# Sums of w_in on VectorE, and the last four rows' states made together from 64-row products

## The chip, the cores and the metric

The kernel runs on one core of a Trainium2 chip. The metric is the device time of one execution in microseconds. The kernel before takes 1135.21 us as the median of three runs (1133.67 to 1135.47). The engines are TensorE (PE in the rows; its weight loads are PEld), VectorE (DVE), ScalarE (ACT), GpSimd (POOL) and SyncE (SP), which issues every DMA here.

## The reference

Attention of every batch row between 512 tokens and 32 states, in both directions, then two feed-forward layers over all 8 x (512 + 32) = 4608 tokens.

```python
B, H, S, Ns, D = (8, 8, 512, 32, 64)
a     = softmax(x @ state.T * scale);   xread = a @ state       # token rows
a2    = softmax(state @ x.T * scale);   sread = a2 @ x          # state rows
x     = concat([xread, sread]) as (4608, 512)
# layer 1: d_ff 1536
gate  = 1.0 / (1.0 + np.exp(-(x @ w_gate)));  val = x @ w_val
x     = (gate * val) @ w_out
# layer 2: d_ff 1024
h     = x @ w_in
solu  = h * softmax(h)
ln    = (solu - mean) / sqrt(var + 1e-06) * g_ln
out   = ln @ w_out2
```

The weights come as 64-bit floats and are turned into 32-bit ones on the chip. A 32-bit operand of a large product is split into a high and a low half, and the product is the sum of three: high by high, low by high, high by low (`mm3`, lines 137 to 140).

## The kernel before

Layer 1 goes through nine token blocks: batch rows 0 to 6, then all 256 state tokens together (the state row, `SREAD`), then batch row 7, the last row. Each block has 12 chunks of 128 hidden units (loop at line 1037). A chunk is 12 products for gate and val into the banks `gps` and `vps` (`first_mm`), a sigmoid on ScalarE (`sigma`), the product of both on VectorE (`gated`), its split into `gh` and `gl`, and 12 products by `w_out` into four banks (`out_acc`), one chunk late. Beside it, attention of the next row runs in ten parts (`attention`); chunk 4 holds its exponentials (`exps`), which switch ScalarE's table and back.

A token row needs no product by w_gate of full depth. Since xread is a by state, `state_w` makes state by weights (256 x 3072 per row) in 12 steps, each 128 x 512 of gate and val of two chunks, and `first_mm` multiplies that by the attention weights. From row 2 on, rows go in pairs (`paired`): while the even row of the pair is made, six products of 128 rows a step (three for each of two groups `k` of 128 weight rows) make both rows' states. Their stationary operand holds two heads and two rows by 32 states, with the two heads' halves swapped between rows. Half of a result belongs to the other row, is copied to SBUF (`spill`) and stored to DRAM (`msp`); the odd row loads its steps from there (`state_load`) and only splits them (`put`). `make` issues a step in each chunk, two or three chunks ahead of use; `loads` issues the loads up to three steps ahead.

The order within this part is the order of the code (`manual_schedule`); each engine runs its own list in that order, and SyncE likewise its DMAs. In the state row `Conv` turns w_in into halves `xe`, `xo`; in the last row it does the same for w_out2 (`conv.step`, lines 1077 and 1078: ScalarE, three VectorE operations, one GpSimd addition `L223`, then a split at `L235`). Also in the last row, two steps a chunk of `w_pair_ops` form T1 to T4 from w_in: `do_join` adds the halves, `do_sub` subtracts, `do_split` splits, all on GpSimd but for the high half on ScalarE.

Layer 2 then runs over 34 tiles of 128 tokens in pairs (lines 1128 to 1180), seven products a pair instead of eight. `turn` transposes a tile through DRAM, `halves` splits it when it has come back, `out2` multiplies by w_out2, `store` writes. In the first pair, ScalarE meets `halves` ahead of the copies of products 5 and 6. In the last pair product 4 overwrites the bank that VectorE's `plus` (line 1164) reads, and that `plus` stands behind `chain(i)`.

The lines printed next are those that the profile names.

Of the kernel before, what the change touches and what calls it, by code (L numbers as in the profile page):

```python
# [9 lines left out]
F32 = mybir.dt.float32  # L10
# [4 lines left out]
ALU = mybir.AluOpType  # L15
# [3 lines left out]
WARM = 11  # L19
EXPS = 7  # L20

EXP_LO = 2.0 ** -15
# [4 lines left out]
def attn_moe_moe2_kernel(ctx: ExitStack, tc: tile.TileContext, x, state, w_gate, w_val, w_out, w_in2, w_out2, g_ln, out):  # L27
# [88 lines left out]
    ysp = [tc.dram_tile([KC, P, S if b < B else SR], F32, name=f"ysp{b}") for b in range(B + 1)]  # L116
    ssp = tc.dram_tile([B, P, KC * NS], F32, name="ssp")
    msp = [tc.dram_tile([NF1, P, 512], F32, name=f"msp{b}") for b in range(B)]

# [171 lines left out]
    def paired(a):  # L291
        return 2 <= a < B and a - a % 2 + 1 < B

# [213 lines left out]
    def state_w(b, p, g, i, o, hi, o2=vps):  # L507
# [3 lines left out]
        s = spill[n % 4]  # L511
        if not paired(b):
# [3 lines left out]
        elif b % 2 == 0:  # L516

            for q, o in enumerate((gps, o2)):
                k = 2 * g + q
                mm3(o, sth[:, k, :], stl[:, k, :], wpart(xe, p, k), wpart(xo, p, k), True, True)  # L520
                own = slice(64 * q, 64 * q + 64)
                other = slice(64 - 64 * q, 128 - 64 * q)
                hi(h[own], o[own])
                hi(s[other], o[other])
                lo_of(l[own], o[own], h[own])
            for q in range(2):
                nc.sync.dma_start(out=msp[b + 1][n, 64 - 64 * q:128 - 64 * q], in_=s[64 * q:64 * q + 64])
        else:
            put(s, h, l, hi)

    def state_load(b, n):
        nc.sync.dma_start(out=spill[n % 4], in_=msp[b][n])

# [37 lines left out]

    def out_acc(c, n):
        h, l = woh[c], wol[c]
        i = c % 2
        for m in range(KC):
            sl = slice(m * P, (m + 1) * P)
# [59 lines left out]
    def w_pair_ops(bf):  # L636

        join, sub, split = [{} for _ in range(3)]
        for k in range(2):
            b = dict(zip(("B11", "B12", "B21", "B22"), bf[4 * k:4 * k + 4]))  # L640

            def do_join(n, k=k, b=b):
                h, l = win(k + 2 * (n[1] == "2"), int(n[2]) - 1)
                pool.tensor_tensor(out=b[n], in0=r(h), in1=r(l), op=ALU.add)

            def do_sub(o, x, y, b=b):
                pool.tensor_tensor(out=b[o], in0=b[x], in1=b[y], op=ALU.subtract)
# [13 lines left out]
        for k in range(2):  # L661
            steps += late[:1] + [join["B11", k], join["B12", k], sub["T1", k], join["B22", k], split["T1", k], sub["T3", k]]
            steps += [sub["T2", k], join["B21", k], split["T3", k], split["T2", k], sub["T4", k]]
            late = [split["T4", k]]
# [11 lines left out]
    def h2_out(i, f):  # L676
        if tiles[i][0] == 0:
            return acc[2 * (i % 2) + f]
        a, b, c = banks(i)
        return ((b, c), (a, b))[i % 2][f]  # L680

# [138 lines left out]
    def make(n=1, o=gps, hi=hi_of, o2=vps):  # L820
        nonlocal made
        while n and made - NF1 < len(ring) and made - used < 3:
            state_w(*ring[made - NF1], made, o, hi, o2)
            made += 1
            n -= 1

    def loads(n):

        nonlocal loaded
        loaded = max(loaded, made - NF1)  # L830
        while loaded < min(made - NF1 + n, len(ring)):
            b, p, g = ring[loaded]
            if not paired(b) or b % 2 == 0:
                return
# [175 lines left out]
    with tc.manual_schedule():  # L1010
        for n_b, b in enumerate(blocks[1:], 1):
# [5 lines left out]
            if last:  # L1017
# [7 lines left out]
                y_load(1)  # L1025
                x_late.close()
                sbt = ctx.enter_context(tc.tile_pool(name="sbt", bufs=1, side="right"))
                for w in ("T1", "T2", "T3", "T4"):
# [6 lines left out]
                w_steps = w_pair_ops([sbf.tile([P, 512], F32, name=f"bf{i}") for i in range(8)])  # L1035
            nxt = blocks[n_b + 1] if not last else None
            for c in range(NF1):
                pe, others = parts[c] if c < len(parts) else (None, None)
# [14 lines left out]
                make(1, hi=hi, o2={3: vps, 4: vps, 7: vps, 9: att[0]}.get(c, att[1]))  # L1053
                if c > 0:
                    out_acc(c - 1, n)
                else:
                    out_acc(NF1 - 1, n_before)
# [21 lines left out]
                if last:  # L1079
                    for _ in range(2):  # L1080
# [46 lines left out]
    with tc.manual_schedule():  # L1127
        for i in range(len(first), nt, 2):
# [15 lines left out]
            h_max(i, 0)  # L1144
            halves(i - 2, 0)
            halves(i - 2, 1)
            row_scale(i - 2)
# [16 lines left out]
            plus(v, o, tmp)  # L1164
            h_max(i + 1, 1)
            centre(i)
# [57 lines left out]
```

## Time and profile before

| | before |
|---|---|
| median of three runs | 1135.21 us |
| the profiled execution's own time | 1134.19 us |
| its span, first to last instruction | 1132.4 us |
| mean granted TensorE clock | 0.994 |
| TensorE busy | 1084.0 us (96%) |
| VectorE busy | 766.7 us (68%) |
| ScalarE busy | 601.8 us (53%) |
| GpSimd busy | 418.7 us (37%) |

A row of a timeline gives the start in us, the duration in us, the engine, the line, the operation, output<-inputs and a count; what stands in brackets is idle time before it and who ended it. Products overlap: their durations are longer than the distance between their starts, so a stretch is read from starts.

### The profile page before, as it was taken

How to read it: one execution, taken by the hardware profiler on the slowest of the kernel's cores; microseconds unless marked ns; L12 is line 12 of the kernel's file. 1: busy time of each engine (PE TensorE's matmuls, PEld its weight loads, DVE VectorE, ACT ScalarE, POOL GpSimd, SP SyncE). 2: the span in 40 equal slices, each digit the busy share in tenths (PEclk: the TensorE clock that was granted, in tenths of full speed). 3: DMA queues.
4: the chain of work that ended last, by engine and by line, in shares of the span. 5: the costliest groups of instructions: out<-in, count | busy, mean ns of one | idle time of the engine just before them, and what ended most of it. 6: DMA issues, size and time to landing. Idle time of an engine off the chain costs nothing.

```text
span 1132.4 us, 15911 instructions
## 1 busy us (share of the span) xinstructions
PE 1084.0 (96%) x5501; PEld 861.5 (76%) x5501; DVE 766.7 (68%) x1324; ACT 601.8 (53%) x1169; POOL 418.7 (37%) x469
## 2 busy tenths in 40 slices
PE   7887899999999999999999999889999999999998
PEld 5555567778878778778778997667788888888877
DVE  6999865467465575564574466877578778777773
ACT  6766445545444455443555354555565565655552
POOL 2776733300000000000000054676566667667550
PEclk9999999999999999999999999999999999999999
DMA  8763040331440431532412434311453543553431
GB/s 230 258 204 102 20 95 1 80 84 38 116 124 20 115 66 38 164 77 58 96 38 67 142 99 149 106 39 56 134 174 121 174 155 131 164 170 119 158 122 38
DMA packets 139601, 122.89 MB, mean 109 GB/s; under 512 B 71040, under 2 KB 111232, under 8 KB 139520
## 3 DMA queue, kind: packets, MB, share of 16 engines
q1 hardware_dynamic: 139520, 121.87, 36.8%
q8 instruction: 43, 0.70, 0.3%
q14 instruction: 38, 0.31, 0.1%
HBM read 78.32 MB, written 43.52 MB: 108 GB/s over the span
## 4 chain that ended last, share of the span: by engine, by line
PE 73%; DVE 14%; issue 3%; DMA 3%; POOL 2%; ACT 2%; SPq 1%; DVEq 0%; POOLq 0%; ACTq 0%
PE acc L138 10%; PE acc L140 10%; PE acc L139 10%; PE att L138 5%; PE att L140 5%; PE att L139 5%; PE gps L138 4%; PE gps L139 4%; PE gps L140 4%; PE vps L138 4%; PE vps L140 4%; PE vps L139 4%; DVE wf L213 2%; DVE wf L203 1%; DVE wf L206 1%
## 5 line engine op out<-in xcount | busy, mean ns | idle before, releaser
L138 PE MATMUL acc<-gh,woh 128*128 128x512 f32 (+1 forms) x432 | 168.7, 390 | 0.6 <-ACT gh L129 0.6
L564 DVE TENSOR_TENSOR sg<-vps,sg 128x512 f32<-128x512 f32 (+1 forms) x108 | 71.1, 658 | 141.7 <-PE vps L140 123.0
L139 PE MATMUL acc<-gl,woh 128*128 128x512 f32 (+1 forms) x432 | 164.6, 381 | 2.2 <-POOL gl L570 1.3
L140 PE MATMUL acc<-gh,wol 128*128 128x512 f32 (+1 forms) x432 | 164.3, 380 | 0.0
L560 ACT ACTIVATE sg<-gps 128x512 f32<-128x512 f32 (+1 forms) x108 | 61.6, 570 | 154.5 <-PE gps L140 150.0
L138 PEld LDWEIGHTS acc<-gh,woh 128*128 128x128 f32 x432 | 81.8, 189 | 31.9 <-issue 15.5
L256 POOL MEMSET xtr<- 32x256 f32 x18 | 5.4, 302 | 262.1 <-PE att L324 261.5
L139 PEld LDWEIGHTS acc<-gl,woh 128*128 128x128 f32 x432 | 81.9, 190 | 18.5 <-POOL gl L570 2.2
L775 POOL TENSOR_TENSOR wol<-ut,woh 128x512 fp32r<-128x512 f32 x48 | 61.6, 1299 | 87.7 <-ACT woh L129 85.8
L140 PEld LDWEIGHTS acc<-gh,wol 128*128 128x128 f32 x432 | 81.6, 189 | 16.1
L223 POOL TENSOR_TENSOR tt<-tt,xn 128x512 int32<-128x512 int32 x16 | 20.9, 1304 | 194.8 <-DVE tt L213 171.2
L129 ACT ACTIVATE gh<-sg 128x512 fp32r<-128x512 f32 (+1 forms) x101 | 60.5, 599 | 53.6 <-DVE sg L564 53.6
L138 PE MATMUL gps<-ah,mh 128*128 128x512 f32 x192 | 75.9, 396 | 9.3 <-ACT sg L560 4.1
L570 DVE TENSOR_TENSOR gl<-sg,gh 128x512 fp32r<-128x512 f32 (+1 forms) x97 | 76.3, 786 | 10.2 <-ACT gh L129 6.9
L135 DVE TENSOR_TENSOR ml<-gps,mh 64x512 fp32r<-64x512 f32 (+2 forms) x57 | 38.6, 678 | 63.1 <-ACT stg L129 51.0
L138 PE MATMUL att<-woh,woh 128*128 128x512 f32 (+1 forms) x204 | 80.1, 392 | 0.0
L139 PE MATMUL att<-wol,woh 128*128 128x512 f32 (+1 forms) x204 | 79.5, 390 | 0.0
L140 PE MATMUL att<-woh,wol 128*128 128x512 f32 (+1 forms) x204 | 79.5, 390 | 0.0
L129 ACT ACTIVATE mh<-gps 64x512 fp32r<-64x512 f32 (+2 forms) x53 | 31.2, 589 | 90.7 <-PE gps L140 60.4
L139 PE MATMUL gps<-al,mh 128*128 128x512 f32 x192 | 75.4, 393 | 1.7 <-DVE al L135 1.7
L138 PE MATMUL vps<-ah,mh 128*128 128x512 f32 x192 | 75.7, 395 | 1.1 <-DVE ml L135 1.1
L140 PE MATMUL gps<-ah,ml 128*128 128x512 f32 x192 | 75.4, 393 | 1.0 <-DVE ml L135 0.9
(431 smaller groups left out, 2900.0 us busy)
## 6 DMA issues: line engine op xcount, KB each, us to landing
usp<-ub SPq DMA_DIRECT2D x32, 512.0 KB, 2.6
ut<-usp SPq DMA_DIRECT2D x128, 128.0 KB, 2.9
msp<-stg SPq DMA_DIRECT2D x72, 128.0 KB, 2.3
stg<-msp SPq DMA_DIRECT2D x36, 256.0 KB, 2.9
out_dram<-sg SPq DMA_DIRECT2D x32, 256.0 KB, 3.0
xn<-in_x_dram SPq DMA_DIRECT2D x15, 512.0 KB, 5.3
e2t<-in_x_dram SPq DMA_DIRECT2D x96, 64.0 KB, 2.6
stge<-in_moe_w_out_dram SPq DMA_DIRECT2D x10, 512.0 KB, 4.0
```

The source lines that it names most:

```text
L129: return act(dst, src, AF.Copy)
L135: return vec.tensor_tensor(out=dst, in0=src, in1=r(hi), op=ALU.subtract)
L138: mm(o, lh, rh, start=start, stop=False, **kw)
L139: mm(o, lh, rl, start=False, stop=False, **kw)
L140: return mm(o, ll, rh, start=False, stop=stop, **kw)
L203: vec.tensor_scalar(out=t, in0=t, scalar1=EXP_LO, scalar2=EXP_HI, op0=ALU.max, op1=ALU.min)
L213: vec.scalar_tensor_tensor(out=tu, in0=hi, scalar=0xC0000000, in1=tu, op0=ALU.bitwise_and, op1=ALU.bitwise_or)
L223: pool.tensor_tensor(out=ti, in0=ti, in1=lo, op=ALU.add)
L560: act(sg[c % 2][:, 0:n], gps[:, 0:n], AF.Sigmoid)
L564: vec.tensor_tensor(out=g, in0=vps[:, 0:n], in1=g, op=ALU.mult)
L570: eng.tensor_tensor(out=gl[c % 2][:, 0:n], in0=sg[c % 2][:, 0:n], in1=r(gh[c % 2][:, 0:n]), op=ALU.subtract)
L775: pool.tensor_tensor(out=lv, in0=wv[:, 4 * q:4 * q + 4], in1=r(hv), op=ALU.subtract)
```

## The change

Rows 4 to 7 no longer go in pairs (`QUAD = 4`). In the last chunk of row 2 their four states, loaded into `qst`, are transposed on TensorE and split (`quad_t`, `quad_split`): `sth` and `stl` now hold, for each group k, two heads in 64 partitions each, by 4 rows x 32 states. `quad_w` multiplies one head at a time: for each of 24 (p, k), six products of 64 rows by 128 x 512, the two heads in turn, each head into a bank of its own. ScalarE copies one result, VectorE the other, and two DMAs store them to `qsp`. That runs in the middle of `out_acc` in all 12 chunks of row 3 (twice in chunks 5, 6, 10 and 11) and in the first 8 of row 4. Every row from 4 on loads each of its steps with four DMAs of 32 partitions, at most two steps ahead.

In the last row `do_join`, `do_sub` and the low half of `do_split` go to VectorE; the low half of a split comes a chunk after the subtraction, and the last split behind the last `out_acc`. In layer 2's first pair `halves` and `row_scale` come after the copies of products 5 and 6. In its last pair `plus` writes to bank `acc[3]` and comes before `chain(i)`.

```diff
     def paired(a):
-        return 2 <= a < B and a - a % 2 + 1 < B
+        return 2 <= a < QUAD
...
     def state_load(b, n):
-        nc.sync.dma_start(out=spill[n % 4], in_=msp[b][n])
+        if b < QUAD:
+            nc.sync.dma_start(out=spill[n % 4], in_=msp[b][n])
+            return
+        p, g = divmod(n, 2)
+        for h in range(4):
+            r0 = NS * (b - QUAD)
+            nc.sync.dma_start(out=spill[n % 4][NS * h:NS * h + NS], in_=qsp[p][4 * g + h, r0:r0 + NS])
...
+    def quad_w(pks, os):
+        hs = [slice(64 * i, 64 * i + 64) for i in range(2)]
+        for (p, k), o2 in zip(pks, os):
+            w1, w2 = wpart(xe, p, k), wpart(xo, p, k)
+            for n, (s, w) in enumerate(((sth, w1), (sth, w2), (stl, w1))):
+                for o, h in zip(o2, hs):
+                    mm(o, s[h, k, :], w[h], start=n == 0, stop=n == 2)
+        for j, ((p, k), o2) in enumerate(zip(pks, os)):
+            for i, o in enumerate(o2):
+                s = spill4[2 * (k % 2) + i]
+                if i == 0:
+                    act(s, o, AF.Copy)
+                else:
+                    vec.tensor_copy(out=s, in_=o)
+                nc.sync.dma_start(out=qsp[p][2 * k + i], in_=s)
...
-                pool.tensor_tensor(out=b[n], in0=r(h), in1=r(l), op=ALU.add)
+                vec.tensor_tensor(out=b[n], in0=r(h), in1=r(l), op=ALU.add)
...
-                pool.tensor_tensor(out=l, in0=b[x], in1=r(h), op=ALU.subtract)
+                vec.tensor_tensor(out=l, in0=b[x], in1=r(h), op=ALU.subtract)
...
+                two = n_b == QUAD - 1 and c in (5, 6, 10, 11)
+                for m in range(0, KC, 2):
+                    if m and (n_b == QUAD - 1 or n_b == QUAD) and quads:
+                        quad_w(*zip(*[(quads.pop(0), o) for o in [(gps, vps), att][:1 + two]]))
+                    if c > 0:
+                        out_acc(c - 1, n, range(m, m + 2))
...
-                    loads(3 if c + 1 < NF1 else 1)
+                    loads(3 if b < QUAD - 1 and c + 1 < NF1 else 2 if c + 1 < NF1 else 1)
...
         out_acc(NF1 - 1, S)
+        w_steps.pop(0)()
...
+            if i > len(first):
+                operand()
             product(i, 5, w, True, False)
             act(tmp, w, AF.Copy)
             product(i, 6, o, False, False)
             act(u2, o, AF.Copy)
+            if i == len(first):
+                operand()
...
             if end:
                 product(i, 7, o, False, False)
+                plus(acc[3], o, tmp)
+                h_max(i + 1, 1)
             chain(i)
```

On TensorE, in a chunk of row 4, the order before has the six products of a step (`xe`, `xo` are the weights' halves, `sth`, `stl` the states') between `first_mm` and `out_acc`:

```order
L140 MATMUL vps<-ah_90,ml 128x512
L138 MATMUL gps<-xe_1535,sth 128x512
L139 MATMUL gps<-xo_1536,sth 128x512
L140 MATMUL gps<-xe_1535,stl 128x512
L138 MATMUL vps<-xe_1535,sth 128x512
L139 MATMUL vps<-xo_1536,sth 128x512
L140 MATMUL vps<-xe_1535,stl 128x512
L138 MATMUL acc_174<-gh_96,woh_68 128x512
```

In the order now they stand between the second and the third bank of `out_acc`, and the two banks alternate:

```order
L140 MATMUL acc_175<-gh_96,woh_66 128x512
L141 MATMUL acc_175<-gl_98,woh_66 128x512
L142 MATMUL acc_175<-gh_96,wol_78 128x512
L563 MATMUL gps<-xe_1665,sth 128x512
L563 MATMUL vps<-xe_1665,sth 128x512
L563 MATMUL gps<-xo_1666,sth 128x512
L563 MATMUL vps<-xo_1666,sth 128x512
L563 MATMUL gps<-xe_1665,stl 128x512
L563 MATMUL vps<-xe_1665,stl 128x512
L140 MATMUL acc_176<-gh_96,woh_66 128x512
L141 MATMUL acc_176<-gl_98,woh_66 128x512
L142 MATMUL acc_176<-gh_96,wol_78 128x512
```

The count of a step is the same, six. Before, the last two chunks of rows 3 and 5 and the first ten of rows 4 and 6 have one step each; now all chunks of row 3 and the first eight of row 4 have one or two, and rows 5 and 6 none.

On ScalarE, from the exponentials of row 3's chunk 4 on, the order before goes from the last of them straight to the next chunk's `sigma` (`sg`):

```order
L371 ACTIVATE ee_106,st_124<-att_181,st_124 128x512
L384 ACT_TABLE_LOAD
L384 ACTIVATE stat_125<-half 128x1
L560 ACTIVATE sg_110<-gps 128x512
L129 ACTIVATE mh<-stg_112 128x512
L129 ACTIVATE gh_96<-sg_110 128x512
```

Now a copy of `gps` to `qst` stands behind the second table load and ahead of that `sigma`:

```order
L599 ACTIVATE sg_110<-gps 128x512
L131 ACTIVATE mh<-stg_112 128x512
L568 ACTIVATE qst_2453<-gps 128x512
L568 ACTIVATE qst<-att_180 128x512
L131 ACTIVATE gh_96<-sg_110 128x512
L599 ACTIVATE sg_109<-gps 128x512
L131 ACTIVATE mh<-stg_111 128x512
```

The bank `gps` is thus free for the next chunk only when the exponentials are through and this copy with them.

On VectorE, in a chunk of the last row, the order before goes from the three operations of `conv.step` to the next `gated`; the sums and T1 to T4 are GpSimd's (two rows of it between two `L223`):

```order
L235 SCALAR_TENSOR_TENSOR wol_77<-tt_103,glnt,woh_65 128x512
L203 TENSOR_SCALAR tt_104<-tt_104 128x512
L206 TENSOR_SCALAR tt_104<-tt_104 128x512
L213 SCALAR_TENSOR_TENSOR tt_104<-xn_100,tt_104 128x512
L564 TENSOR_TENSOR sg_109<-vps,sg_109 128x512
```

```order
L223 TENSOR_TENSOR tt_103<-tt_103,xn_99 128x512
L652 TENSOR_TENSOR T3l_5308<-bf_5331,T3h_5307 128x512
L652 TENSOR_TENSOR T2l_5304<-bf_5333,T2h_5303 128x512
L223 TENSOR_TENSOR tt_104<-tt_104,xn_100 128x512
```

Now two of them stand between `L215` (line 213 before) and that `gated`:

```order
L237 SCALAR_TENSOR_TENSOR wol_78<-tt_104,glnt,woh_66 128x512
L205 TENSOR_SCALAR tt_103<-tt_103 128x512
L208 TENSOR_SCALAR tt_103<-tt_103 128x512
L215 SCALAR_TENSOR_TENSOR tt_103<-xn_99,tt_103 128x512
L683 TENSOR_TENSOR bf_5426<-xe_1210,xo_1211 128x512
L691 TENSOR_TENSOR T2l_5398<-bf_5427,T2h_5397 128x512
L603 TENSOR_TENSOR sg_110<-vps,sg_110 128x512
L137 TENSOR_TENSOR ml<-stg_112,mh 128x512
```

GpSimd keeps only the addition of `conv.step`, and its order in this row is one addition after the other.

## Rows read from the trace of the kernel before

**Rows 1.** The page, busy time, share of the span and count by engine.

```profile
PE 1084.0 (96%) x5501; PEld 861.5 (76%) x5501; DVE 766.7 (68%) x1324; ACT 601.8 (53%) x1169; POOL 418.7 (37%) x469
```

**Rows 2.** Timeline, TensorE: first product of rows 3, 4, 5, 6 and the state row.

```profile
309.92 0.39 PE L138 MATMUL gps<-ah,mh 128*128 128x512 f32 x1
...
383.96 0.39 PE L138 MATMUL gps<-ah,mh 128*128 128x512 f32 x1
...
469.61 0.39 PE L138 MATMUL gps<-ah,mh 128*128 128x512 f32 x1
...
543.65 0.39 PE L138 MATMUL gps<-ah,mh 128*128 128x512 f32 x1
...
629.30 0.28 PE L138 MATMUL gps<-ah,xe 128*128 128x256 f32 x1
```

**Rows 3.** Same view: two neighbouring chunk starts without making, two with it.

```profile
335.04 0.39 PE L138 MATMUL gps<-ah,mh 128*128 128x512 f32 x1
...
340.48 0.39 PE L138 MATMUL gps<-ah,mh 128*128 128x512 f32 x1
...
399.50 0.39 PE L138 MATMUL gps<-ah,mh 128*128 128x512 f32 x1
...
406.38 0.39 PE L138 MATMUL gps<-ah,mh 128*128 128x512 f32 x1
```

**Rows 4.** Groups by line, weight loads: count, busy us, mean ns.

```profile
L139 PEld LDWEIGHTS acc<-gl,woh 128*128 128x128 f32 x432 | 81.9, 190 | 18.5 <-POOL gl L570 2.2 <-DVE gl L570 1.6
```

**Rows 5.** Timeline, TensorE: a chunk with column-tiled products; a window closing at 206.645.

```profile
168.20 0.39 PE L138 MATMUL gps<-ah,mh 128*128 128x512 f32 x1
...
171.01 1.08 PE L514 MATMUL gps<-wf,stt 128*64 128x512 f32 x4
...
174.88 0.39 PE L138 MATMUL gps<-ah,mh 128*128 128x512 f32 x1
...
206.64 0.65 PE L514 MATMUL gps<-wf,stt 128*64 128x512 f32 x2
```

**Rows 6.** Timeline, ScalarE, row 3, chunk 4: first of the exponentials, next sigma.

```profile
337.28 1.28 ACT L355 ACT_TABLE_LOAD   x1
...
342.46 0.58 ACT L560 ACTIVATE sg<-gps 128x512 f32<-128x512 f32 x1
```

**Rows 7.** Timeline, TensorE, from 727 on: products with idle time before them.

```profile
727.48 0.50 PE L138 MATMUL gps<-ah,mh 128*128 128x512 f32 x1 [4.07 <-ACT sg L560]
...
747.70 0.50 PE L140 MATMUL gps<-ah,ml 128*128 128x512 f32 x1 [0.87 <-DVE ml L135]
...
765.03 0.50 PE L138 MATMUL acc<-xe,mh 128*128 128x512 f32 x1 [2.97 <-DVE ml L135]
...
806.87 0.50 PE L138 MATMUL acc<-xe,ys5h 128*128 128x512 f32 x1 [1.14 <-ACT stg L1149]
...
1103.78 0.52 PE L138 MATMUL acc<-T4h,mh 128*128 128x512 f32 x1 [2.10 <-DVE acc L696]
```

**Rows 8.** Stretches of TensorE: length, busy, count, granted clock, DMA share, GB/s.

```profile
727.50:731.00 3.50, 3.50 (x11) 0.67 0.46 119
766.40:769.30 2.90, 2.90 (x8) 0.50 0.00 0
1104.20:1107.50 3.30, 3.30 (x9) 0.50 0.00 0
```

**Rows 9.** Timeline, ScalarE, last row.

```profile
726.31 0.63 ACT L129 ACTIVATE T4h<-bf 128x512 fp32r<-128x512 f32 x1 [6.26 <-POOL bf L647]
```

**Rows 10.** Timeline, VectorE, last row: one subtraction twice, two starts of a gate.

```profile
728.85 0.69 DVE L570 TENSOR_TENSOR gl<-sg,gh 128x512 fp32r<-128x512 f32 x1
...
733.71 1.79 DVE L570 TENSOR_TENSOR gl<-sg,gh 128x512 fp32r<-128x512 f32 x1
...
738.64 0.68 DVE L564 TENSOR_TENSOR sg<-vps,sg 128x512 f32<-128x512 f32 x1
...
745.58 0.69 DVE L564 TENSOR_TENSOR sg<-vps,sg 128x512 f32<-128x512 f32 x1
```

More of the change, by code (lines that the diff above doesn't have):

```diff
@@ L117, in attn_moe_moe2_kernel @@
     ssp = tc.dram_tile([B, P, KC * NS], F32, name="ssp")
+    qsp = [tc.dram_tile([H, P, 512], F32, name=f"qsp{p}") for p in range(NF1 // 2)]
     msp = [tc.dram_tile([NF1, P, 512], F32, name=f"msp{b}") for b in range(B)]
@@ L511, in state_w @@
         s = spill[n % 4]
-        if not paired(b):
+        if b < 2:
             for q in range(2):
@@ L515, in state_w @@
             put(o, h, l, hi)
-        elif b % 2 == 0:
+        elif b < QUAD and b % 2 == 0:
             for q, o in enumerate((gps, o2)):
@@ L531, in state_load, with quad_load, quad_t, quad_split @@
     def state_load(b, n):
-        nc.sync.dma_start(out=spill[n % 4], in_=msp[b][n])
+        if b < QUAD:
+            nc.sync.dma_start(out=spill[n % 4], in_=msp[b][n])
+            return
+        p, g = divmod(n, 2)
+        assert not quads or quads[0] > (p, 2 * g + 1)
+        for h in range(4):
+            r0 = NS * (b - QUAD)
+            nc.sync.dma_start(out=spill[n % 4][NS * h:NS * h + NS], in_=qsp[p][4 * g + h, r0:r0 + NS])
+    def quad_load():
+        for a in range(QUAD, B):
+            r0 = NS * (a - QUAD)
+            nc.sync.dma_start(out=qst[r0:r0 + NS].rearrange("n (h d) -> n h d", h=H), in_=state[a].rearrange("h n d -> n h d"))
+    def quad_t(o):
+        for k in range(KC):
+            nc.tensor.transpose(o[:, k * P:(k + 1) * P], qst[:, k * P:(k + 1) * P], ident)
+    def quad_split(o):
+        put(o, *[x.rearrange("p k n -> p (k n)") for x in (sth, stl)])
+    def quad_w(pks, os):
[13 more added lines that the diff above has]
+                nc.sync.dma_start(out=qsp[p][2 * k + i], in_=s)
     def state_w1(c, o=gps, t=slice(0, 2), hi=hi_of):
@@ L570, in gated_lo, with out_acc @@
         eng.tensor_tensor(out=gl[c % 2][:, 0:n], in0=sg[c % 2][:, 0:n], in1=r(gh[c % 2][:, 0:n]), op=ALU.subtract)
-    def out_acc(c, n):
+    def out_acc(c, n, ms=range(KC)):
         h, l = woh[c], wol[c]
         i = c % 2
-        for m in range(KC):
+        for m in ms:
             sl = slice(m * P, (m + 1) * P)
@@ L661, in w_pair_ops @@
         for k in range(2):
-            steps += late[:1] + [join["B11", k], join["B12", k], sub["T1", k], join["B22", k], split["T1", k], sub["T3", k]]
-            steps += [sub["T2", k], join["B21", k], split["T3", k], split["T2", k], sub["T4", k]]
+            steps += [join["B11", k], *late, join["B12", k], sub["T1", k], join["B22", k], sub["T3", k], split["T1", k]]
+            steps += [sub["T2", k], split["T3", k], join["B21", k], split["T2", k], sub["T4", k]]
             late = [split["T4", k]]
@@ L679, in h2_out @@
         a, b, c = banks(i)
-        return ((b, c), (a, b))[i % 2][f]
+        return ((b, c), (a, acc[3] if i + 1 == len(tiles) else b))[i % 2][f]
     def product(i, n, o, start, stop):
@@ L825, in make @@
             n -= 1
+    quads = [(p, k) for p in range(NF1 // 2) for k in range(KC)]
     def loads(n):
@@ L832, in loads @@
             b, p, g = ring[loaded]
-            if not paired(b) or b % 2 == 0:
+            if b < 2 or paired(b) and b % 2 == 0:
                 return
@@ L1036, in attn_moe_moe2_kernel @@
             nxt = blocks[n_b + 1] if not last else None
+            if n_b == 2:
+                q_pool = ExitStack()
+                sbq = q_pool.enter_context(tc.tile_pool(name="sbq", bufs=1))
+                qst = sbq.tile([P, 512], F32, name="qst")
+                quad_load()
+            if n_b == 3:
+                spill4 = [qst, *[sbq.tile([P, 512], F32, name=f"qst{i}") for i in range(3)]]
             for c in range(NF1):
@@ L1053, in attn_moe_moe2_kernel @@
                 make(1, hi=hi, o2={3: vps, 4: vps, 7: vps, 9: att[0]}.get(c, att[1]))
[L1054 to L1057, printed above, removed]
+                if n_b == 2 and c == NF1 - 1:
+                    quad_t(att[0])
+                    quad_split(att[0])
+                two = n_b == QUAD - 1 and c in (5, 6, 10, 11)
[4 more added lines that the diff above has]
+                        out_acc(c - 1, n, range(m, m + 2))
+                    else:
+                        out_acc(NF1 - 1, n_before, range(m, m + 2))
                 gated_hi(c, n, hi)
@@ L1079, in attn_moe_moe2_kernel @@
                 if last:
-                    for _ in range(2):
+                    for _ in range(min(2, len(w_steps) - 1)):
                         w_steps.pop(0)()
@@ L1144, in attn_moe_moe2_kernel, with operand @@
             h_max(i, 0)
-            halves(i - 2, 0)
-            halves(i - 2, 1)
-            row_scale(i - 2)
+            def operand():
+                halves(i - 2, 0)
+                halves(i - 2, 1)
+                row_scale(i - 2)
+            if i > len(first):
+                operand()
             product(i, 5, w, True, False)
@@ L1163, in attn_moe_moe2_kernel @@
                 product(i, 7, o, False, False)
-            plus(v, o, tmp)
-            h_max(i + 1, 1)
+            if not end:
+                plus(v, o, tmp)
+                h_max(i + 1, 1)
             centre(i)
```

4 lines of the change are left out of this document (3 added, 1 removed).

## Prediction

> **What bounds the kernel now.** I read the page first: TensorE is busy for 1084.0 of 1132.4 us [rows 1], so time goes only with its products or with its few gaps. Then its timeline, in starts. A chunk of 24 products without making takes 340.48 - 335.04 = 5.44 us, 0.227 us a product; one with a step of making takes 406.38 - 399.50 = 6.88 us, so six products of 128 rows cost 1.44 us [rows 3]. The starts of the rows say the same from further off: row 4, with ten steps, takes 85.65 us and row 3, with two, 74.04 us [rows 2], 1.45 us for each of eight steps. There TensorE waits for nobody: taking products out shortens the kernel, and what other engines do beside it counts only if it makes TensorE wait. Next the idle times in brackets. From the last row on there are five of a size that matters [rows 7]: 4.07, 0.87, 2.97, 1.14 and 2.10 us. Last the granted clock behind the long ones: 0.67 over 3.5 us, 0.50 over 2.9 us and 0.50 over 3.3 us, where 1.0 is 2.4 GHz and 0.50 is 1.2 GHz [rows 8]. At half clock half of a stretch is lost: 1.2, 1.4 and 1.6 us on top of the three long gaps.
>
> **The states' products.** Removed are 24 steps (ten and two chunks, twice) at 1.44 us: 34.6 us. Added are 144 products of 64 rows in 24 groups of six. No row of before has two halves of rows at work together. It has the like in columns: two products of 64 columns both start by 206.645, 5 ns after the first at 206.64 [rows 5], so they run side by side. Bounds for a pair of 64-row products: 0.227 us if the halves run side by side too, 0.454 us if they take turns, and 0.83 us if each also waits for its weights (0.19 us [rows 4] and 0.227 us, twice). I take 0.227, since the column pair is the nearest row.
>
> A change between 128-row and other tile shapes has its price. The chunk with four column-tiled records takes 174.88 - 168.20 = 6.68 us, 1.24 more than 5.44; two pairs at 1.08 - 0.65 = 0.43 us are 0.87 of it [rows 5], so going in and out costs 0.37. There are 20 visits: 16 with one group (3 x 0.227 + 0.37 = 1.05 us) and 4 with two (1.73 us), together 23.7 us. A visit at no cost would make it 16.3.
>
> The Trainium skill, TensorE: Matmul & The Clock Gate, section "Measured speedup vs the span model", gives 3.07 times for four row tiles instead of four. No run here shows it. Read as 77% of the ideal it would make a pair 0.30 us, the sum 5 us larger, as an estimate from that page.
>
> The copies: each group adds one copy on ScalarE and one on VectorE, and takes away half-copies of the pairs. They lie beside six products of `out_acc` (1.36 us) and cost nothing, but for chunk 4. There the copy of `gps` stands behind the exponentials, and ScalarE is through with them only when the next sigma starts, at 342.46; with 0.58 us for the copy the bank is free at 343.0 [rows 6]. TensorE wants it at 340.48 plus the visit's 1.05, at 341.5. So 1.5 us in row 3 and the same in row 4: 3.0 us. If ScalarE were done sooner it would be 0.
>
> The DMAs: 48 stores and 48 groups of four loads instead of 72 and 36. SyncE holds them in order, and a store that waits for chunk 4's copy holds up the loads behind it; they are two steps ahead, two chunks or 11 us, so I count 0, and one chunk's wait (1.5 us) as the upper end. Four transposes with their split come in row 2 and eight smaller ones go: 0.
>
> States together: -34.6 + 23.7 + 3.0 = -7.9 us.
>
> **The last row.** The 4.07 us gap is ScalarE's: its sigma stood behind T4's high half, which had waited 6.26 us for GpSimd [rows 9]. With the subtractions on VectorE and a chunk ahead of their split, that wait goes, and with it 4.07 + 1.2 + 0.87 = 6.1 us. What is late next is VectorE. Its chunk took 745.58 - 738.64 = 6.94 us, since an operation beside a GpSimd one takes 1.79 us instead of 0.69 [rows 10]: 1.10 us lost for each of three GpSimd operations a chunk. Now it is one, and two operations of 0.69 come in: 6.94 - 2.2 + 1.4 = 6.1 us against TensorE's 5.44. It falls back 0.7 us a chunk, over seven chunks with full load 4.9. Before, it fell back 1.5 a chunk over three chunks and TensorE waited 0.87 [rows 7], so about 3.6 are free. New wait 1.2 us, between 0 and 3: -4.9 us.
>
> Behind the last row, 2.97 + 1.4 = 4.4 us go with T4's late split. In its place ScalarE has the table load (1.28 us [rows 6]) and T4's high half (0.63 [rows 9]) after the last `gh`, then VectorE two operations of 0.69 [rows 10]: 3.3 us. TensorE has 0.69 and twelve products, 3.4 us. This is about even; I count 0.7 us of wait: -3.7 us.
>
> **Layer 2.** In the first pair the copy no longer waits behind `halves`: 1.14 us go, and I count 0.1 for `halves` being later: -1.0. In the last pair 2.10 + 1.6 us go, since `plus` is through before TensorE has done the `out2` between: -3.7. What follows on VectorE and ScalarE moves with TensorE and stays level with it.
>
> **Sum.** -7.9 - 4.9 - 3.7 - 1.0 - 3.7 = -21.2 us. The profiled execution has 1134.19 us (span 1132.4, 1.8 around it) and would have 1113.0; the median of the runs shown is 1.0 above it, so 1114 us.
>
> **The rivals.**
> *Halves in turn.* A pair takes 0.454 us: 72 x 0.227 = 16.3 us more, 1130 us, and the states alone lose 8 us. For it: no row shows row halves together. Against it: column halves do run together, and the halves here go to different banks.
> *Weights not hidden.* Each pair waits for a load of 0.19 us: 13.7 us more, 1128 us. In 128-row products a load of 0.19 lies wholly inside a spacing of 0.227, which speaks against it. The Trainium skill, same page, section "The mechanism", states that a load overlaps running products only where the row group differs. By that rule loads would be seen here; the trace's 0.227 of full-height products disagrees.
> *VectorE becomes the bound of the last row.* If it loses 1.10 us to GpSimd twice a chunk, it falls back 1.8 us a chunk, 12.6 in seven, of which 3.6 are free: 9.0 us of wait instead of 1.2, 1122 us.
> *Slower.* Product and load one after the other, 0.417 us each, without overlap of halves: 144 x 0.417 + 20 x 0.37 = 67.4 instead of 23.7, 1158 us. It decides the sign: with the other terms at -13.3, -34.6 and 3.0 + 7.4, the change loses from 0.26 us a product on its own. The full-height spacing of 0.227, which already hides the load, is near that point but below it.
>
> **How the numbers follow.** Forecast 68% (1106 to 1119: visits at half their price and no wait in chunk 4 below, a few us of waits above), halves in turn 10%, weights not hidden 6%, VectorE 9%, slower 5%, and 2% that another wait eats it all. The range reaches from 1103 (visits for nothing, and no new wait in the last row) to 1130. A difference of 0.2%, 2.3 us, is about what a measurement tells from none. All cases but the last two are faster by more: 0.93; within 0.02; slower 0.05.
>
> **What would show it.** Right: in rows 3 and 4 the two 64-row products of a pair start within some ns, a visit adds about 1.05 us to a chunk of 5.44, rows 5 and 6 have chunks of 5.44 throughout, the gap of 4.07 is gone and VectorE's chunk in the last row is near 6.1 us, the clock stays at 1.0 at the end. Wrong: starts of a pair 0.2 us apart, loads between products, bracketed waits on `qst` copies in chunks other than 4, or on `stg` loads.

## The result, and the profile of the changed kernel

The changed kernel takes 1123.25 us (median of 4 runs, 1122.95 to 1123.62), the kernel before 1134.44 beside it: a ratio of 0.9903, 95% interval 0.9886 to 0.9921. It is faster, and the time lies in the wide range (1103 to 1130) and above the 1106 to 1119 that had 68%: the gain is 11.2 us where 21.2 were forecast. Half of the forecast is missing, and the rest of this text is about where that half went.

The page, in the line of [rows 1] (engine, busy time, share of the span, instructions); the span is 1121.2 us:

```profile
PE 1075.8 (96%) x5497; PEld 841.0 (75%) x5497; DVE 764.1 (68%) x1335; ACT 576.7 (51%) x1120; POOL 383.4 (34%) x441
```

TensorE's busy time fell by 8.2 us (half-clock stretches counted), the span by 11.2.

Next, the timeline of TensorE (start, duration, engine, line, operation, tiles, count, idle time before it and what ended it). Of row 3 the starts of chunks 2, 3, 4 and 5 and a double visit; then row 4, row 5, the state row, the last row and layer 2.

```profile
325.13 0.39 PE L140 MATMUL gps<-ah,mh 128*128 128x512 f32 x1
...
331.70 0.39 PE L140 MATMUL gps<-ah,mh 128*128 128x512 f32 x1
...
339.49 0.39 PE L140 MATMUL gps<-ah,mh 128*128 128x512 f32 x1
...
347.55 0.50 PE L140 MATMUL gps<-ah,mh 128*128 128x512 f32 x1 [1.32 <-ACT qst L568]
...
359.12 0.50 PE L563 MATMUL gps<-xe,sth 64*128 64x512 f32 x1
359.12 0.50 PE L563 MATMUL vps<-xe,sth 64*128 64x512 f32 x1
359.46 0.40 PE L563 MATMUL gps<-xo,sth 64*128 64x512 f32 x1
...
359.70 0.39 PE L563 MATMUL gps<-xe,stl 64*128 64x512 f32 x1
...
360.71 0.50 PE L140 MATMUL acc<-gh,woh 128*128 128x512 f32 x1
...
415.20 0.51 PE L140 MATMUL gps<-ah,mh 128*128 128x512 f32 x1 [0.80 <-ACT qst L568]
...
500.04 0.39 PE L140 MATMUL gps<-ah,mh 128*128 128x512 f32 x1
...
507.84 0.39 PE L140 MATMUL gps<-ah,mh 128*128 128x512 f32 x1
...
625.76 0.28 PE L140 MATMUL gps<-ah,xe 128*128 128x256 f32 x1
...
645.10 0.38 PE L140 MATMUL gps<-ah,xe 128*128 128x256 f32 x1 [0.81 <-ACT sg L599]
...
683.88 0.39 PE L140 MATMUL gps<-ah,mh 128*128 128x512 f32 x1
...
730.41 0.50 PE L142 MATMUL gps<-ah,ml 128*128 128x512 f32 x1 [1.60 <-DVE ml L137]
...
743.43 0.50 PE L142 MATMUL gps<-ah,ml 128*128 128x512 f32 x1 [1.60 <-DVE ml L137]
...
757.24 0.50 PE L140 MATMUL acc<-xe,mh 128*128 128x512 f32 x1
...
775.21 0.50 PE L140 MATMUL acc<-xe,mh 128*128 128x512 f32 x1 [0.90 <-DVE xn L758]
...
891.94 0.50 PE L142 MATMUL att<-woh,wol 128*128 128x512 f32 x1 [0.64 <-POOL wol L814]
...
1094.26 0.40 PE L140 MATMUL acc<-T4h,mh 128*128 128x512 f32 x1
```

- Chunk 2 with a single visit takes 331.70 - 325.13 = 6.57 us, against 5.44 without [rows 3]: a visit costs 1.13. Chunk 4 takes 347.55 - 339.49 = 8.06, since its copy to `qst` comes late.
- The two halves of 64 rows run together: the two first products start within the same 10 ns. All twelve products of the double visit take 360.71 - 359.12 = 1.59 us, 0.13 each, where a product of 128 rows takes 0.227 [rows 3]. With the way in, the chunk is longer by 1.80: it takes 7.24 us instead of 5.44.
- The chunk that began at 500.04 takes 507.84 - 500.04 = 7.80 us; before, a chunk of this kind without making takes 6.68. So row 5 is not free of waits, though none stands on a `qst` copy there.
- The state row takes 683.88 - 625.76 = 58.12 us from its first product to the last row's. (The expectation of e_w_in_first below gives 62.97 and 59.7 for this stretch; these run on to the last row's second chunk, and the first chunk is 4.85 of either.)
- The gaps of 4.07, 2.97, 1.14 and 2.10 us of [rows 7] are gone: the products of 757.24 and 1094.26, which answer to 765.03 and 1103.78, have no bracket. New are 1.60 us twice on `ml`, 0.90 at 775.21 on `xn` and 0.64 at 891.94 on `wol`.

The products of 757.24 and 1094.26 stand in full-clock stretches, where [rows 8] had 0.50 (length, busy and count of PE, PEld, DVE, ACT and POOL, granted clock, DMA share, GB/s):

```profile
1092.00:1096.00 4.00, 4.00 (x19) 3.29 (x18) 3.09 (x6) 2.49 (x6) 0.66 (x1) 1.00 0.21 65
757.00:760.00 3.00, 3.00 (x14) 2.27 (x13) 1.98 (x4) 2.79 (x8) 1.59 (x3) 1.00 0.01 3
```

What TensorE waits for in rows 4 to 6 and the state row is found one engine back. Timeline of SyncE's queue in the changed kernel; the duration of a group of DMAs is what their issue took together:

```profile
410.42 5.67 SPq L541 DMA_DIRECT2D stg<-qsp  x12
...
490.42 5.68 SPq L541 DMA_DIRECT2D stg<-qsp  x12
496.15 4.23 SPq L280 DMA_DIRECT2D e2t<-in_x_dram  x6
...
632.62 6.41 SPq L541 DMA_DIRECT2D stg<-qsp  x12
639.08 0.90 SPq L181 DMA_DIRECT2D xn<-in_moe_w_in_dram  x2
```

And those who waited for them, VectorE in row 5 and ScalarE in row 4 and in the state row:

```profile
501.16 0.71 DVE L322 STREAM_TRANSPOSE xtr<-e2t 128x512 f32<-128x512 f32 x1 [1.20 <-DMA e2t<-in_x_dram]
...
414.03 0.63 ACT L131 ACTIVATE mh<-stg 128x512 fp32r<-128x512 f32 x1 [5.38 <-DMA stg<-qsp]
...
643.56 0.66 ACT L197 ACTIVATE tt<-xn 128x512 f32<-128x512 f32 x1 [3.98 <-DMA xn<-in_moe_w_in_dram]
```

Twelve loads of 64 KB hold SyncE for 5.67 us, 0.47 each. Twelve are three steps: `loads(3)` after a row's first chunk is as before the change, so "at most two steps ahead" does not hold there. In row 4 the states themselves are late: ScalarE stands 5.38 us on `stg`, and the copy that TensorE waits for at 415.20 stands behind that. In row 5 `load_xq` stands behind the twelve. In the state row the first loads of `w_in` do: they leave 13.3 us after the row's first product (639.08 - 625.76). In the kernel before, two loads of `stg<-msp` stood there, and `w_in` left 7.9 us after the row's start (637.22 - 629.30 [rows 2]):

```profile
636.17 0.95 SPq L532 DMA_DIRECT2D stg<-msp  x2
637.22 0.84 SPq L179 DMA_DIRECT2D xn<-in_moe_w_in_dram  x2
```

### The profile page after: what moved, and what is told of

The parts are those of the page before. It is cut to its first block, busy times and chain, and to the rows that moved or that the text cites. A ratio compares the mean times of both kernels' runs of the same rounds, so it can differ in the third digit from the quotient of the medians.

```text
span 1121.2 us, 16144 instructions
## 1 busy us (share of the span) xinstructions
PE 1075.8 (96%) x5497; PEld 841.0 (75%) x5497; DVE 764.1 (68%) x1335; ACT 576.7 (51%) x1120; POOL 383.4 (34%) x441
## 4 chain that ended last, share of the span: by engine, by line
PE 68%; DVE 15%; DMA 5%; issue 4%; SPq 3%; ACT 3%; POOL 1%; POOLq 0%; ACTq 0%; DVEq 0%
PE acc L140 10%; PE acc L142 9%; PE acc L141 9%; PE att L142 5%; PE att L140 5%; PE att L141 5%; PE gps L140 4%; PE vps L140 4%; PE vps L142 4%; PE vps L141 4%; PE gps L141 3%; PE gps L142 3%; DVE wf L215 2%; DVE wf L205 2%; DVE wf L208 1%
## 5 line engine op out<-in xcount | busy, mean ns | idle before, releaser
L140 PE MATMUL acc<-gh,woh 128*128 128x512 f32 (+1 forms) x432 | 171.7, 398 | 0.2 <-ACT gh L131 0.2
L225 POOL TENSOR_TENSOR tt<-tt,xn 128x512 int32<-128x512 int32 x16 | 23.5, 1468 | 202.5 <-DVE tt L215 192.9
L609 DVE TENSOR_TENSOR gl<-sg,gh 128x512 fp32r<-128x512 f32 (+1 forms) x97 | 68.6, 707 | 17.6 <-ACT gh L131 14.0
L142 PE MATMUL vps<-ah,ml 128*128 128x512 f32 x192 | 74.8, 390 | 0.0
L141 PE MATMUL vps<-al,mh 128*128 128x512 f32 x192 | 74.8, 390 | 0.0
```

The costliest lines, as they stand in the source:

```text
L140: mm(o, lh, rh, start=start, stop=False, **kw)
L141: mm(o, lh, rl, start=False, stop=False, **kw)
L142: return mm(o, ll, rh, start=False, stop=stop, **kw)
L225: pool.tensor_tensor(out=ti, in0=ti, in1=lo, op=ALU.add)
L609: eng.tensor_tensor(out=gl[c % 2][:, 0:n], in0=sg[c % 2][:, 0:n], in1=r(gh[c % 2][:, 0:n]), op=ALU.subtract)
```

## The experiments

**Theory.** The states' part is right on TensorE and wrong on SyncE: four DMAs for a step instead of one stand ahead of other work in an ordered queue, and the price is the waits above. **Rivals:** the visits cost more than thought; the bytes, not the issues, are the cost; the missing time is in the last row or in layer 2.

**The change in its parts.** b_sums is the kernel before with the hunks on `w_pair_ops` and the last row's spread alone; b_end has the hunks on `banks` and on the order of layer 2's pairs alone:

```diff
-                pool.tensor_tensor(out=b[n], in0=r(h), in1=r(l), op=ALU.add)
+                vec.tensor_tensor(out=b[n], in0=r(h), in1=r(l), op=ALU.add)
...
-        return ((b, c), (a, b))[i % 2][f]
+        return ((b, c), (a, acc[3] if i + 1 == len(tiles) else b))[i % 2][f]
```

> The kernel before with one part of the change alone: the sums of w_in on VectorE and their order and spread over the chunks of the last row. By the trace of the changed kernel this part gives 3.4 in the last row and 4.7 behind it, less what returns in layer 2. Theory: 7 to 9 less than the kernel before (1134.5), 1126 to 1128, if the new waits of layer 2 (0.9 to 1.15 at three places) come from where layer 2 now starts against its DMAs; rival (they come from the other parts): 1125 to 1126, with layer 2 unchanged.

> The kernel before with one part of the change alone: the order of the first pair of layer 2 and the earlier sum and other bank of the last pair. The prediction's terms are 1.0 and 3.7, the trace of the changed kernel shows 1.0 and 4.0. Theory: 4.5 to 5.2 less than the kernel before, 1129.3 to 1130. Rival: the last pair only gains because its clock no longer falls with the rest of the change, 1131 to 1133.

b_sums: 1126.51 us, 0.9927 (0.9909 to 0.9945) of the kernel before, 8.5 us less by the medians. b_end: 1129.67, 0.9964 (0.9947 to 0.9981), 5.3 less. Both medians are as expected. The interval of b_end reaches into its rival's range, but its trace has 3.9 us less in the last pair without the rest of the change. The two medians add up to 13.8, more than the 11.2 of the whole change, which would leave nothing for the states. The same from the other side, the changed kernel without the states' part; in the first of the two the last pair's last product stood in another bank than the one that its sum read, so its last tile was another value:

> The changed kernel without the part on the last four rows' states (they are made as before, two rows at a time, 128 rows a product); the sums on VectorE and the end stay. The two parts alone gave 8.5 and 5.3 less than the kernel before, the whole change 11.2. Theory: the states' part, forecast at 7.9 less, costs about as much as it gives or more, because its DMAs hold up the w_in loads of the state row (3.3 by the trace) and rows 4 to 6 (3): 1120 to 1122. Rival (the two other parts do not add up, and the states give their 3.8 of rows 3 to 6 or more): 1125 to 1131.

> The changed kernel without the states' part, as a_no_states, now with the last pair's last product in the bank that the changed kernel gives it (in a_no_states that product stood in the other bank while its sum read this one, so its last tile was another value). Theory: 1120 to 1122.5, as there, or up to 1 less: the states' part of the changed kernel gives between nothing and a loss of 3. Rival: the bank alone is worth 2 or more, and the states with it a loss of 3 to 5 (1118 to 1120); or the states give their 3.8 of rows 3 to 6 after all (1126 to 1128).

Measured: 1122.04 (0.9896, 0.9881 to 0.9910), and with the right bank 1124.33 (0.9914, 0.9897 to 0.9931). The changed kernel has 0.9903. So the two other parts together give 11.4 and 9.9, not surely the 13.8 of their sum, and the states' part, forecast at a gain of 7.9 us, is worth a loss of 1.2 or a gain of 1.1 by the medians. With both intervals it lies between a gain of some 4 and a loss of some 1.5 against the second of the two: half of the forecast at the most. The timeline of TensorE in b_sums gives the state row without the states' loads, and with it the price there:

```profile
628.86 0.28 PE L138 MATMUL gps<-ah,xe 128*128 128x256 f32 x1
...
683.73 0.39 PE L138 MATMUL gps<-ah,mh 128*128 128x512 f32 x1
```

54.87 us, 3.3 less than in the changed kernel (b_end 54.84, a_no_states_bank 54.81). The kernel before has 684.72 - 629.30 = 55.42 in its profiled execution; since b_end, with the sums still on GpSimd, has 54.84, these 0.6 us are not the sums'. What the sums do give is 1.0 us in the last row's first chunk, for which nothing was forecast: it takes 5.86 before and 5.81 in b_end, 4.84 in b_sums and 4.85 in the changed kernel. Before, TensorE waits there for VectorE, which works beside GpSimd's sums:

```profile
687.20 0.50 PE L139 MATMUL gps<-al,mh 128*128 128x512 f32 x1 [0.73 <-DVE al L135]
```

**Do halves run together only because their products alternate?** e_in_turn:

```diff
-            for n, (s, w) in enumerate(((sth, w1), (sth, w2), (stl, w1))):
-                for o, h in zip(o2, hs):
+            for o, h in zip(o2, hs):
+                for n, (s, w) in enumerate(((sth, w1), (sth, w2), (stl, w1))):
```

> The changed kernel with the three products of one 64-row half issued before the three of the other. If the halves overlap only because their instructions alternate, each of the 24 pairs of three costs 3 x 0.23 us more, 24 x 0.69 = 16.6 us: 1138 to 1141. Rival (the two halves do not share the array, and the equal starts in the trace are a modelled artefact): within 1 us of 1123. A third outcome, 1128 to 1135, would mean that the engine overlaps the last of one half with the first of the other.

1123.86 us (0.9909, 0.9889 to 0.9929): no change, but not for the rival's reason. Timeline of TensorE, the same double visit; its code has three products to `gps` ahead of the first to `vps`:

```profile
359.20 0.50 PE L563 MATMUL gps<-xe,sth 64*128 64x512 f32 x1
359.21 0.50 PE L563 MATMUL vps<-xe,sth 64*128 64x512 f32 x1
...
360.81 0.50 PE L140 MATMUL acc<-gh,woh 128*128 128x512 f32 x1
```

The twelve products take 1.61 us, against 1.59: the fourth in the code starts with the first. The time is the rival's, its reason is not: twelve products one after the other would take 2.7 us at 0.227, so the halves do share the array, and it takes no alternation. The theory's 16.6 us fall. By the trace a visit costs 1.13 us, and so the part of the miss that lies in the visits is 20 times 0.08, 1.6 us.

**Number of issues against bytes.** e_eight_loads halves each load, with the same bytes:

```diff
-            nc.sync.dma_start(out=spill[n % 4][NS * h:NS * h + NS], in_=qsp[p][4 * g + h, r0:r0 + NS])
+            for f in (slice(0, 256), slice(256, 512)):
+                nc.sync.dma_start(out=spill[n % 4][NS * h:NS * h + NS, f], in_=qsp[p][4 * g + h, r0:r0 + NS, f])
```

> The changed kernel with each of the four loads of a step split in two halves of 256 columns: eight DMAs a step, the same bytes. Theory (SyncE's issue): 192 more issues of some 0.47 us, of which the waits of rows 4 to 6 and of the state row grow: 12 loads after a chunk become 24 and take 11.3 us, so each of the four places loses some 3 to 6 us more, 1133 to 1145. Rival (bytes): 1123 to 1125.

1152.89 us (1.0158, 1.0139 to 1.0178), 29.6 more than the changed kernel, beyond the expectation's range, which had one delay at each place. Timeline of TensorE in row 6, where the delay now meets both kinds of consumer:

```profile
584.03 0.50 PE L140 MATMUL gps<-ah,mh 128*128 128x512 f32 x1 [1.15 <-ACT mh L131]
...
595.57 1.31 PE L326 MATMUL att<-xtr,stt 128*64 128x512 f32 x2 [3.48 <-DVE xtr L322]
```

The bytes as rival are out. The other direction, one DMA for four heads, e_one_load:

```diff
-        for h in range(4):
-            r0 = NS * (b - QUAD)
-            nc.sync.dma_start(out=spill[n % 4][NS * h:NS * h + NS], in_=qsp[p][4 * g + h, r0:r0 + NS])
+        r0 = NS * (b - QUAD)
+        nc.sync.dma_start(out=spill[n % 4], in_=qsp[p][4 * g:4 * g + 4, r0:r0 + NS])
```

> The changed kernel with one DMA for a step's four heads instead of four DMAs of 32 partitions; bytes and order are the same. Theory (SyncE's issue): twelve loads hold the queue for 5.7 us in the changed kernel, so three would hold it for some 1.4 us; the waits for DMAs in chunk 3 of rows 5 and 6 (1.1 and 1.0 us), in chunk 1 of row 4 (1.0) and the late start of the state row's conversion chain (2 to 2.7) go: 4 to 6 us less than the changed kernel's 1123.25, so 1117 to 1119. Rival (the bytes or the dearer visits are the cost): within 1 us of 1123.

1138.1 us (1.0030, 1.0019 to 1.0041): 15 slower, where 4 to 6 faster was expected. The issue did become cheap, 0.53 us a step. But the transfer became slow. A stretch of e_one_load with nothing in flight but loads of this form (columns as above):

```profile
475.00:476.50 1.50, 1.50 (x9) 1.23 (x8) 0.00 (x0) 0.54 (x2) 0.00 (x0) 1.00 0.26 101
```

A share of 0.26 of 16 engines is four of them, and 101 GB/s is what they move; 256 KB would then take 2.6 us, and three loads issued together 7.8. ScalarE in row 4 and TensorE behind it:

```profile
421.51 0.63 ACT L131 ACTIVATE mh<-stg 128x512 fp32r<-128x512 f32 x1 [8.69 <-DMA stg<-qsp]
```

```profile
422.68 0.51 PE L140 MATMUL gps<-ah,mh 128*128 128x512 f32 x1 [4.11 <-ACT qst L567]
```

The Trainium skill, DMA: Bandwidth & Descriptors, section "Why a DMA increments its semaphore by 16 and not by 1", states that a DMA runs on as many engines, up to 16, as divide the slowest dimension of both its patterns. Here it is 4 in memory and 128 in the buffer, so the page gives four engines, and the trace agrees with 0.26. e_by_row moves the same pattern to the stores: memory is laid out row by row, a step's load is one plain DMA, and the store scatters.

```diff
-        for h in range(4):
-            r0 = NS * (b - QUAD)
-            nc.sync.dma_start(out=spill[n % 4][NS * h:NS * h + NS], in_=qsp[p][4 * g + h, r0:r0 + NS])
+        nc.sync.dma_start(out=spill[n % 4], in_=qsp[p][g, b - QUAD])
...
-                nc.sync.dma_start(out=qsp[p][2 * k + i], in_=s)
+                r0 = NS * (2 * (k % 2) + i)
+                nc.sync.dma_start(out=qsp[p][k // 2, :, r0:r0 + NS], in_=s)
```

> The changed kernel with the states in memory row by row: a step's load is one plain DMA of 128 partitions, and the store of a half of 64 rows (48 in all) is the one that scatters, four outer blocks of 32 partitions. The run with one load for four heads showed that a DMA of four outer blocks moves about 100 GB/s, where others move 400; 256 KB then take 2.6 us. Theory: 192 issues become 48 and the slow pattern sits on stores, for which nobody waits but their own buffers, two visits later: the waits in rows 4 to 6 and the state row's late start go, 4 to 6 less, 1117 to 1119. Rival (the slow stores hold up what is behind them, as the slow loads did): 1125 to 1140.

1143.92 us (1.0089, 1.0067 to 1.0111): the rival, 20.7 more. Rows 5 and 6 have no waits in it, but in rows 3 and 4 the stores come so late that the copies wait for their buffers (timeline of ScalarE, then of TensorE):

```profile
410.41 0.60 ACT L566 ACTIVATE qst<-gps 128x512 f32<-128x512 f32 x1 [9.39 <-DMA qsp<-qst]
```

```profile
411.06 0.79 PE L140 MATMUL gps<-ah,mh 128*128 128x512 f32 x1 [6.05 <-ACT qst L566]
```

**The order on SyncE.** e_behind puts `load_xq` (rows 5 and 6) and the first loads of `w_in` (state row) ahead of the states; e_w_in_first moves the latter alone:

```diff
                     y_spill(before, n_before, b)
+                    if b == SREAD:
+                        conv = Conv(...)
+                        conv.load()
+                        conv.load()
+                    if n_b > QUAD and parts:
+                        load_xq(n_b + 1, 1)
                     loads(3)
-                    if parts:
+                    if n_b <= QUAD and parts:
                         load_xq(n_b + 1, 1)
```

> The changed kernel with the same DMAs in another order on SyncE: in rows 5 and 6 load_xq, and in the state row the first loads of w_in, stand ahead of the loads of the next states instead of behind them. Theory (order on SyncE's queue, not bytes): the waits of rows 5 and 6 (1.1 and 1.0) go and the state row's conversion chain starts some 5 us earlier (2 or more): 3 to 5 less, 1118 to 1120.5; if the states, which now come 4 us later, are waited for, some of it returns. Rival (bytes in flight): within 1 us of 1123.

> The changed kernel with one move on SyncE: in the state row the first two loads of w_in stand ahead of the twelve loads of states, not behind them. Theory: the state row, 62.97 from its first product to that of the last row in the trace of the changed kernel, comes back to the 59.7 that it has with the sums alone, 3 less: 1119.5 to 1121. Rival (the conversion chain is late for its own work or for bytes): 1122.5 to 1123.5.

e_behind: 1130.05 us (0.9957, 0.9943 to 0.9971), 7 slower than the changed kernel instead of 3 to 5 faster. The chunk of row 5 that took 7.80 us takes 6.68 again, but the one ahead of it now waits for its state (timeline of TensorE):

```profile
500.19 0.79 PE L140 MATMUL gps<-ah,mh 128*128 128x512 f32 x1 [3.61 <-ACT mh L131]
```

So a mere exchange turns one wait into a longer one. e_w_in_first has a state row of 54.74 us in its profiled execution, as long as without the states' part. That is 3.4 us less, as expected, and that execution took 1120.00. But the median is 1123.80 (0.9911, 0.9892 to 0.9929): its six runs go from 1120.00 to 1126.72, and which waits the longer ones have, one profile does not show. In the time this run is inconclusive.

**Chunk 4.** e_chunk4_vec takes both copies of chunk 4 on VectorE:

```diff
-                if i == 0:
+                if i == 0 and not on_vec:
                     act(s, o, AF.Copy)
```

> The changed kernel with both copies of the products in chunk 4 (the chunk with the exponentials) on VectorE instead of one on ScalarE behind the exponentials. Theory: the wait of 1.32 us at the next write of that bank goes in rows 3 and 4, 2 x 1.4 = 2.8 us less, some 1120.5; if VectorE's second copy makes its own work late, some of it returns (1121 to 1122). Rival (another wait lies just behind it): within 0.5 us of 1123.

1120.90 us (0.9880, 0.9861 to 0.9899), 2.4 less. The product that stood at 347.55 stands at 346.30 without a bracket, in a chunk of 6.56 us instead of 8.06.

**All of it.** e_ordered has e_chunk4_vec and the order of e_behind, with the loads of two steps (8 DMAs) ahead of the spill of y in rows 4 to 6, so that no state comes late:

```diff
+                    if QUAD <= b < B - 1:
+                        loads(2)
                     y_spill(before, n_before, b)
```

> The changed kernel with the order on SyncE mended in three places and the copies of chunk 4 on VectorE: in rows 4 to 6 the loads of two steps ahead of the spill of y, in rows 5 and 6 load_xq ahead of the third step's loads, in the state row the w_in loads ahead of the states'. Bytes and number of DMAs are those of the changed kernel. Theory: 2.4 (chunk 4) + 3.3 (state row) + 2.1 (rows 5 and 6) + 0.8 (row 4) = 8.6 less than 1123.25, some 1114.6; 1113.5 to 1117 with what layer 2 takes back. Rival (192 DMAs of 64 KB cost by their number wherever they stand): 1118 to 1121.

1114.73 us (1113.79 to 1116.38), 0.9836 (0.9821 to 0.9851): 8.5 less than the changed kernel by the medians and 7.6 by the two ratios to the kernel before, where 8.6 was expected, and faster than both kernels. Chunk 4 has 2.4 of it, so some 6 us are the order's. DMAs and bytes are those of the changed kernel. TensorE's timeline: the chunk of row 5, then the state row.

```profile
496.03 0.39 PE L140 MATMUL gps<-ah,mh 128*128 128x512 f32 x1
...
502.71 0.39 PE L140 MATMUL gps<-ah,mh 128*128 128x512 f32 x1
...
619.66 0.28 PE L140 MATMUL gps<-ah,xe 128*128 128x256 f32 x1
...
674.38 0.39 PE L140 MATMUL gps<-ah,mh 128*128 128x512 f32 x1
```

The chunk is back at 6.68 us and the state row at 54.72.

## Why the prediction was half right

Term by term, forecast against measured, in us:

| Term | Forecast | Measured | From |
|---|---|---|---|
| Steps away, visits in | -10.9 | -9.3 | visits of 1.13 and 1.80 |
| Chunk 4's copy | +3.0 | +3.0 | 8.06 against 6.56, twice |
| SyncE's DMAs, rows 4 to 6 | 0 | +3.0 | 0.97 + 1.12 + 0.96, chunks against e_ordered |
| SyncE's DMAs, state row | 0 | +3.3 | 58.12 against 54.87 |
| State row, not by the change | none | -0.6 | 54.87 against 55.42 |
| Sums, last row's first chunk | none | -1.0 | 4.84 against 5.86 |
| Last row, the rest | -4.9 | -2.6 | drift of its products |
| Behind the last row | -3.7 | -4.9 | the same |
| Layer 2, its new waits | none | +3.3 | 1.2 at 775.21, then small ones |
| Layer 2, first pair | -1.0 | -1.3 | drift |
| Last pair | -3.7 | -3.9 | drift |

"Drift" is the start of a product after less that of the same product before, at the two ends of the stretch. Drifts are of one profiled execution each; differences of some 0.5 us, as in the state row, come without a change.

**The step that failed** is "they are two steps ahead, two chunks or 11 us, so I count 0, and one chunk's wait (1.5 us) as the upper end". It looked at the states' own lateness alone, and put that at 0. In rows 5 and 6 and in the state row the price, 5.3 of 6.3 us, came from what is *behind* them in the queue: `load_xq` and the loads of `w_in`, which are not two steps ahead of anything. In row 4, 1.0 us, the states themselves were late: after a row's first chunk none is two steps ahead, the burst of 410.42 has to bring them. 192 loads at 0.47 us are 90 us of SyncE instead of 36 loads, after a row's first chunk in bursts of twelve. e_eight_loads shows that the number of issues sets the price, e_ordered that the place in the queue decides whether it is paid. A wait on `stg` loads was on the list of what would show the forecast wrong.

**Visits**: the mechanism was right (pairs together, weights hidden, price for changing shape), the price 0.07 to 0.08 too low each time: 1.13 and 1.80 instead of 1.05 and 1.73, 1.6 us over 20. It lies in two starts on the way in and two on the way out, 0.32 to 0.34 us apart instead of 0.227 (358.80, 359.12, 359.46 and 360.39, 360.71, 361.05); on both ways the first weight load starts with its product instead of 0.23 us ahead of it. The rivals "halves in turn" and "weights not hidden" fell with the first rows of the trace. By the Trainium skill, TensorE: Matmul & The Clock Gate, section "The mechanism", loads would show between one pair and the next, which use the same halves; the trace's spacing of 0.24 (359.46 to the next pair at 359.70) disagrees.

**Chunk 4** came as worked out, 1.5 us twice, and e_chunk4_vec shows that it could be had back.

**Last row**: VectorE was taken as 6.1 us a chunk. It takes 742.10 - 735.59 = 6.51 (timeline of VectorE, two starts of a gate, as in [rows 10]):

```profile
735.59 0.68 DVE L603 TENSOR_TENSOR sg<-vps,sg 128x512 f32<-128x512 f32 x1
...
740.38 1.80 DVE L691 TENSOR_TENSOR T1l<-bf,T1h 128x512 fp32r<-128x512 f32 x1
742.10 0.68 DVE L603 TENSOR_TENSOR sg<-vps,sg 128x512 f32<-128x512 f32 x1
```

The term that was mis-sized is "1.10 us lost for each of three GpSimd operations a chunk". In the chunk before, `gl` lost 1.10 [rows 10], but the two others less:

```profile
739.24 1.49 DVE L135 TENSOR_TENSOR ml<-stg,mh 128x512 fp32r<-128x512 f32 x1
...
742.36 1.78 DVE L235 SCALAR_TENSOR_TENSOR wol<-tt,glnt,woh 128x512 fp32r<-128x512 f32 x1
```

Now `ml` takes 0.67 and `wol` 0.75, so 0.8 + 1.0 = 1.8 us go instead of 2.2, and 6.94 - 1.8 + 1.4 is 6.5. One operation a chunk still meets GpSimd (1.80 us instead of 0.68). At 6.51 VectorE sets the pace of the last row and TensorE waits 1.60 us in every other chunk. This is the rival "VectorE becomes the bound" in a mild form: 3.2 us of waits, where 1.2 and 9.0 were the two cases. That the measured 1123 us is near the 1122 of this rival is chance; most of the miss lies in the states.

**Sums as a whole**: forecast -8.6, alone -8.5 by the medians, with an interval of some 6 to 10. From the last row's first product on, the profiled execution of b_sums gains 7.7. The last row as a whole gave 1.3 less than forecast and 1.2 were lost at 775.21, against 1.2 more behind the last row. That the total fits so well is luck: a sum that fits does not prove its terms.

**The end and the first pair** came as worked out: -4.7 forecast, -5.3 in b_end, -5.2 in the changed kernel. What stays open are 1.9 of the 3.3 us in layer 2: small waits (0.64 at 891.94 on `wol`, 0.38 at 903.16 on `stg`). The stretch in which they stand takes 14.5 to 15.7 us in all nine profiled runs with the states' part and 13.5 in all five without, so they come with that part, though it ends long before. They begin at a store and a load of `turn` on SyncE's queue, here of the changed kernel:

```profile
878.56 0.38 SPq L802 DMA_DIRECT2D usp<-ub  x1
...
885.50 1.75 SPq L804 DMA_DIRECT2D ut<-usp  x4
```

The load waits until the store has landed and leaves 6.9 us after it; in the nine runs it is 5.7 to 7.2, in the five 4.0 to 5.0. Why the store lands later was not tried.

## What to carry to other kernels

Where a change trades one DMA for four, count the issues on the queue and look at what stands behind them there, not only at the transfer itself; here waits of this kind took 6.3 of the 7.9 us forecast for the states, and another order on the queue gave some 6 back. Before merging DMAs to save issues, look at the outermost dimension of the pattern: four blocks of 32 partitions ran at 101 GB/s. And split a change into its parts before believing a total: two of the three parts together were worth as much as the whole.

## What the runs showed of the hardware

- Two products of 64 rows on different halves of the array start together even when two others of the first half stand between them in the code (359.20 and 359.21 us in e_in_turn).
- A DMA issue on SyncE took 0.47 us for 64 KB (twelve in 5.67), 0.48 for a plain load of 256 KB (two in 0.95 at 636.17, before) and 0.53 for 256 KB in four blocks: the number counts, hardly the size. 192 more issues of the same bytes cost 29.6 us, 0.15 us of the kernel's time for each.
- The wait of 3.61 us in e_behind was followed by half clock, as two of the long gaps of [rows 8] were: such a wait costs more than its length. The 3.0 us behind it in e_behind (columns as in [rows 8]):

```profile
500.20:503.20 3.00, 3.00 (x7) 2.38 (x8) 2.93 (x5) 1.58 (x3) 0.00 (x0) 0.50 0.48 137
```

Granted clock 0.50, 1.2 GHz: half of these 3.0 us is lost on top of the wait.
